# A fourth buffer for float64 words, shared with the later pairs' sums over slots, a third for k's x, one instead of two for turned q: linear attention and an ELU MLP in one launch

## The chip, the cores and the metric

One Trainium2 chip, one core of it. The metric is the device time of one execution in microseconds (us). Nothing is read from an earlier launch; the float64 weights are converted within the launch.

## The reference, cut to what matters

```
def _attn_ref(q, k, v, omega):                 # q, k, v: 8 x 8 x 576 x 64, omega: 128 x 64
    def phi(x):
        proj = np.einsum('bhsd,md->bhsm', x, omega)
        sq = np.sum(x * x, axis=-1, keepdims=True) / 2.0
        h = proj - sq
        h = h - np.max(h, axis=-1, keepdims=True)
        return np.exp(h) / np.sqrt(m)
    q_p, k_p = phi(q * scale), phi(k * scale)
    kv = np.einsum('bhsm,bhsd->bhmd', k_p, v)
    z = np.sum(k_p, axis=2)
    num = np.einsum('bhsm,bhmd->bhsd', q_p, kv)
    den = np.einsum('bhsm,bhm->bhs', q_p, z)[..., None] + 1e-06
    return num / den
...
    x = attn_out.transpose(0, 2, 1, 3).reshape(4608, 512)
    h = x @ w_in                               # 512 x 2048, float64
    g = np.where(h > 0.0, h, np.exp(np.minimum(h, 0.0)) - 1.0)
    return g @ w_out                           # 2048 x 512, float64
```

## The kernel before, in words

Attention is done in 32 **pairs**: a pair is two heads of one batch, so four pairs make a batch of 576 tokens by 512 features. For a pair, `load_pair` has SyncE (SP) load k's x, q's x and v; `project` makes projections on TensorE (PE; `ppk`, `ppq`), takes the least value of each token on VectorE (DVE; `mnk`, `mnq`) and the exponentials on ScalarE (ACT; `hk`, `hq`); `kv` multiplies hk by v on PE (`pkv`); `finish` makes the denominators (PE `pz`, then DVE `junk`, `den`), scales hq by them (the **norm**, L350, on GpSimd, POOL, or on DVE), turns hq on PE (`pt`), copies the turned q to SBUF on ACT (`qh`), multiplies by kv on PE (`pn`) and writes the result as a high part `xh` (ACT) and a low part `xl` (DVE). Pairs 0 to 6 have k in one layout ("native": the squares are taken on the chip by `xk` operations), pairs 7 on have k's x "mixed", where DVE, POOL and ACT split it into `tk` (two halves of 64x576 each) and DVE sums its squares (`sqk`); q's x goes the same way, mixed from pair 8 on (`tq`, `sqq`).

The MLP runs over 12 **blocks** of 384 tokens. A **step** is one of 16 slices of the 2048 inner features for one block: layer 1 is twelve matmuls into the PSUM bank `ph_F` (four chunks of 128 features, each w_high·x_high, w_high·x_low, w_low·x_high; L830 to L832), ACT takes relu and exp (L839, L840), DVE forms `e` (L843), a high and a low part `g` are split off, and layer 2 is nine matmuls (L864 to L866). A chunk is one pair of the batch. Steps 0 to 7 take block 0, for which pairs 0 to 3 must be done; steps 8 to 15 take block 1, half of whose tokens are of batch 1, so that a step's last chunk needs pair 7's xh and xl. `ph` has two banks, shared with other small products, so that layer 1 of step F+2 waits until `e` of step F has been read out of its bank.

The weights come as float64 words. `from_f64` does one 128x512 block in nine instructions: SP loads the words (`raw_w`, L752), ACT makes `u_w` of the upper words (L755) and scales the lower ones (L759), DVE clamps (L763), shifts (L770) and puts in the sign (L775), POOL adds the lower words (L778), a cast makes the high part (`w1c` or `w2h`) and POOL or DVE the low part. There are 16 blocks for each matrix, done for blocks w1_0, w2_0, w1_1 and so on before the steps that need them, mostly before 216 us. `u_w` has three buffers, `raw` three.

The order of all instructions on all engines is made by a planner (`Plan`): each operation has a due time and a planned cost, and whatever is ready, has a buffer and is due first starts next. Buffers of a tag are given out in the order of due times. An operation with an alternative engine goes to whichever would end it first by plan. So a count of buffers changes not only when a tile can be written but the order in which every engine's queue is filled. Names below: `e_7` is `e` of step 7, `tk_8` is tk of pair 8, `u_w2_6` is u of block 6 of the second matrix; a further number is that of the tile.

Of the kernel before, what the change touches and what calls it, by code (L numbers as in the profile page):

```python
# [18 lines left out]
P = 128  # L19
B, H, S, D, M = 8, 8, 576, 64, 128  # L20
# [258 lines left out]
def act(n, psum=False, ptr=False):  # L279
    return (51 if psum else 93) + 0.833 * n + (93 if ptr else 0)  # L280
# [6 lines left out]
def pool(n):  # L287
    return 40 + 2.33 * n
# [3 lines left out]
def performer_elu_kernel(  # L292
# [14 lines left out]
    nc = tc.nc  # L307
# [3 lines left out]
    sb = ctx.enter_context(tc.tile_pool(name="sb", bufs=1))  # L311
# [31 lines left out]
    def copy(e, dst, src):  # L343
        if e == "ACT":
            nc.scalar.copy(dst, src)  # L345
        else:
            nc.vector.tensor_copy(dst, src)  # L347
# [47 lines left out]
    def load_pair(i, due):  # L395
        s = st.setdefault(i, {})

        def dma(dst, src, nbytes, *writes):
            nonlocal due
            op("SP", 500, due, lambda: nc.sync.dma_start(dst(), src), (), writes, nbytes)  # L400
            due += 0.01

        for nm, nat, mixed in (("k", k, kx), ("q", q, qx)):
            if native(i, nm):
                t = s["x" + nm] = Buf(sb, [P, 2, S], F32, "ld" if nm == "k" else "t", f"x{nm}_{i}", 2)
                dma(lambda t=t: t()[0:D], nat[i], P * S * 4, (t, 0), (t, 1))
            else:
                t = s["x" + nm] = Buf(sb, [P, 2, S], F32, "ld", f"x{nm}_{i}", 2)
                dma(lambda t=t: t(), mixed[i - NNAT[nm]], P * S * 8, (t, 0), (t, 3))
        t = s["v"] = Buf(sb, [P, NV], F32, "v", f"v_{i}", 2)  # L410
        dma(lambda: t(), v[i], P * NV * 4, t)
# [168 lines left out]
    def kv_sums(i, due, p, parts):  # L580

        s = st[i]
        h, v, kvf = s["hk"], s["v"], kvs[i % 2]
        z = s["z"] = Buf(sb, [P, 4, M], F32, "zs", f"zs_{i}", 2)
        kvt = Buf(sb, [P, M], F32, "kvt", f"kvt_{i}", 2)

        def mms():
            for t in range(5):
                for a in range(2):
                    j, o = (2 * t + a, (2 * t + a) * (D + 1)) if t < 4 else (8, 8 * (D + 1) + a * (D + 2))  # L590
                    nc.tensor.matmul(  # L591
                        p()[a * D:a * D + D, 0:M], v()[:, o:o + D], h()[:, j, :], start=(t == 0), stop=(t == 4)
                    )

        op("PE", 1260, due, mms, [*parts, v], ((p, 0),))
        op(
            "ACT", act(M, True), due + 2.2, lambda e: copy(e, kvt(), p()[:, 0:M]), ((p, 0),), (kvt,),
            alt=other("kv", "DVE", dve(M)),
        )
        op("PE", 109, due + 2.5, lambda: nc.tensor.transpose(p()[:, M:2 * M], kvt(), ident), (kvt,), ((p, 1),))  # L600
        op(
            "ACT", act(P, True), due + 2.8, lambda e: copy(e, kvf, p()[:, M:2 * M]), ((p, 1),), (("kvf", i % 2),),
            alt=other("kv", "DVE", dve(P)),
        )

        def add(n, d, dst, x, y, reads):
            op("POOL", pool(n), d, lambda: nc.gpsimd.tensor_tensor(dst(), x(), y(), ALU.add), reads, (z,))

        add(4 * M, due + 0.1, lambda: z(), lambda: h()[:, 0:4], lambda: h()[:, 4:8], parts)
        add(2 * M, due + 0.2, lambda: z()[:, 0:2], lambda: z()[:, 0:2], lambda: z()[:, 2:4], (z,))  # L610
        for a in range(2):
            r = slice(a * D, a * D + D)
            add(
                M, due + 0.3 + 0.1 * a, lambda r=r, a=a: z()[r, a], lambda r=r, a=a: z()[r, a],
                lambda r=r: h()[r, 8], [*parts, z],
            )

    def finish(i, due):
# [11 lines left out]
                nc.tensor.transpose(pz()[:, a * P:(a + 1) * P], z()[:, a:a + 1].to_broadcast([P, P]), ident)  # L630

        def sums():
            nc.tensor.matmul(pz()[:, 0:2 * M], ones, z()[:, 0:2].rearrange("p a m -> p (a m)"), start=True, stop=True)  # L633

        if i < NONES:
            op("PE", 220, due - DUE_Z, spread, (z,), (pz,))
        else:
            op("PE", 430, due - DUE_Z, sums, (z,), (pz,))
        qh = Buf(sb, [P, 2, S], F32, "qh", f"qh_{i}", 2)
        for g in range(3):  # L640
            d = due - 9 + g
            js = slice(4 * g, min(4 * g + 4, NJ))
# [86 lines left out]
    def from_f64(src, hi, lo, nm, due, key):  # L729

        raw = Buf(sb, [P, 2 * 512], I32, "raw", f"raw_{nm}", 3)
        u = Buf(sb, [P, 512], F32, "u", f"u_{nm}", 3)

        def words():  # L740
# [12 lines left out]
        op(
            "ACT", act(512), due - 7,
            lambda: nc.scalar.activation(u(), up().bitcast(F32), AF.Copy, scale=2.0 ** -112), ((raw, 1),), (u,),  # L755
        )
        op(
            "ACT", act(512), due - 6.5,
            lambda: nc.scalar.activation(low(), low().bitcast(U32), AF.Copy, scale=2.0 ** -29), ((raw, 0),), ((raw, 0),),  # L759
        )  # L760
        op(
            "DVE", dve(512, True), due - 6,
            lambda e: (nc.vector if e == "DVE" else nc.gpsimd).tensor_scalar(  # L763
                u(), u(), -F64_MAX, F64_MAX, ALU.max, ALU.min
            ),
            (u,), (u,), alt=other("conv_clamp", "POOL", 1885), port=True,
        )
# [248 lines left out]
```

## Time and profile before

| | us |
|---|---|
| median of 3 runs | 1079.98 (1079.9 to 1080.02) |
| the profiled execution's own time | 1078.17 |
| its span, first to last instruction | 1076.3 |
| PE busy in the span | 1050.0 |
| DVE, ACT, POOL busy | 601.5, 731.6, 474.4 |

The span leaves 1.87 us outside the first and last instruction, and the profiled execution is 1.81 us below the median. PE is busy for 98% of the span. In the forty slices of the page PE shows lower digits in the first six slices alone (to about 160 us), and the granted clock is below full there too. The mean clock over the span is 0.990 of 2.4 GHz. What an engine was waiting for is put down by the view of waits to whatever released it last.

### The profile page before, as it was taken

How to read it: one execution, taken by the hardware profiler on the slowest of the kernel's cores; microseconds unless marked ns; L12 is line 12 of the kernel's file. 1: busy time of each engine (PE TensorE's matmuls, PEld its weight loads, DVE VectorE, ACT ScalarE, POOL GpSimd, SP SyncE). 2: the span in 40 equal slices, each digit the busy share in tenths (PEclk: the TensorE clock that was granted, in tenths of full speed). 3: DMA queues.
4: the chain of work that ended last, by engine and by line, in shares of the span. 5: the costliest groups of instructions: out<-in, count | busy, mean ns of one | idle time of the engine just before them, and what ended most of it. 6: DMA issues, size and time to landing. Idle time of an engine off the chain costs nothing.

```text
span 1076.3 us, 19179 instructions
## 1 busy us (share of the span) xinstructions
PE 1050.0 (98%) x6043; PEld 916.2 (85%) x6043; DVE 601.5 (56%) x2343; ACT 731.6 (68%) x1949; POOL 474.4 (44%) x466
## 2 busy tenths in 40 slices
PE   7999699999999999999999999999999999999998
PEld 7777589898888888998888888898888888898987
DVE  5788889755776754235666665224566665322221
ACT  6987775547977985347889998427899988432222
POOL 4677666753443554223454345223344554322221
PEclk8999899999999999999999999999999999999999
DMA  6555477657553553435455545444545542253431
GB/s 196 155 178 191 166 255 258 227 211 234 187 194 128 185 170 128 166 118 168 170 169 156 170 150 177 149 135 134 180 138 177 167 153 98 98 167 131 153 125 62
DMA packets 53237, 176.92 MB, mean 164 GB/s; under 512 B 6032, under 2 KB 6224, under 8 KB 53136
## 3 DMA queue, kind: packets, MB, share of 16 engines
q1 hardware_dynamic: 53136, 175.69, 49.3%
q8 instruction: 49, 0.80, 0.3%
q14 instruction: 52, 0.43, 0.1%
HBM read 155.48 MB, written 20.19 MB: 163 GB/s over the span
## 4 chain that ended last, share of the span: by engine, by line
PE 83%; ACT 5%; DVE 5%; DMA 3%; POOL 2%; issue 2%; SPq 0%; POOLq 0%; DVEq 0%; ACTq 0%
PE acc L864 12%; PE ph L830 11%; PE acc L866 11%; PE acc L865 11%; PE ph L832 11%; PE ph L831 11%; PE ppq L507 2%; PE pt L673 2%; PE pkv L591 2%; PE pn L700 2%; PE ppk L507 2%; DMA xk<-in_kx_dram 1%; PE ppq L457 1%; ACT hk L427 1%; ACT hq L427 1%
## 5 line engine op out<-in xcount | busy, mean ns | idle before, releaser
L350 POOL TENSOR_TENSOR g<-e,g 128x384 fp32r<-128x384 f32 x176 | 186.4, 1059 | 450.5 <-DVE g L347 333.3
L830 PE MATMUL ph<-xh,w1c 128*128 128x384 f32 x768 | 266.6, 347 | 0.8 <-DVE e L843 0.8
L832 PE MATMUL ph<-xh,w1c 128*128 128x384 f32 x768 | 258.3, 336 | 0.0
L831 PE MATMUL ph<-xl,w1c 128*128 128x384 f32 x768 | 258.0, 336 | 0.0
L843 DVE SCALAR_TENSOR_TENSOR e<-e,ph 128x384 f32<-128x384 f32 x192 | 106.2, 553 | 247.5 <-ACT e L840 244.0
L839 ACT ACTIVATE e<-ph 128x384 f32<-128x384 f32 x192 | 94.7, 493 | 216.1 <-PE ph L832 209.7
L864 PE MATMUL acc<-w2h,g 128*128 128x512 f32 x576 | 235.1, 408 | 0.7 <-ACT o L345 0.7
L865 PE MATMUL acc<-w2l,g 128*128 128x512 f32 x576 | 228.3, 396 | 0.0
L866 PE MATMUL acc<-w2h,g 128*128 128x512 f32 x576 | 228.2, 396 | 0.0
L830 PEld LDWEIGHTS ph<-xh,w1c 128*128 128x128 f32 x768 | 144.5, 188 | 15.6 <-issue 5.1
L831 PEld LDWEIGHTS ph<-xl,w1c 128*128 128x128 f32 x768 | 144.6, 188 | 8.0
L832 PEld LDWEIGHTS ph<-xh,w1c 128*128 128x128 f32 x768 | 144.0, 188 | 0.0
L866 PEld LDWEIGHTS acc<-w2h,g 128*128 128x128 f32 x576 | 108.6, 189 | 25.7
L864 PEld LDWEIGHTS acc<-w2h,g 128*128 128x128 f32 x576 | 108.6, 189 | 17.6 <-issue 4.1
L865 PEld LDWEIGHTS acc<-w2l,g 128*128 128x128 f32 x576 | 108.9, 189 | 11.7
L840 ACT ACTIVATE e<-e 128x384 f32<-128x384 f32 x192 | 101.6, 529 | 3.4
L525 DVE CUSTOM_DVE_ANT_0 hq<-ppq,p2q 128x128 f32<-128x128 f32 x216 | 54.1, 288 | 63.4 <-ACT p2q L516 62.4
L350 POOL TENSOR_TENSOR hq<-hq,den 128x512 f32<-128x512 f32 (+1 forms) x93 | 81.0, 884 | 10.2 <-DVE den L661 8.5
L525 DVE CUSTOM_DVE_ANT_0 hk<-ppk,p2k 128x128 f32<-128x128 f32 x225 | 56.3, 287 | 45.6 <-ACT p2k L516 41.1
L652 DVE CUSTOM_DVE_ANT_0 junk<-hq,pz 128x128 f32<-128x128 f32 (+1 forms) x320 | 73.5, 280 | 10.6 <-PE pz L633 8.2
L516 ACT ACTIVATE p2q<-ppq,sqq 128x128 f32<-128x128 f32 x216 | 67.5, 369 | 14.0 <-PE ppq L507 13.3
L516 ACT ACTIVATE p2k<-ppk,sqk 128x128 f32<-128x128 f32 x225 | 67.4, 365 | 7.1 <-PE ppk L507 6.9
(94 smaller groups left out, 1619.5 us busy)
## 6 DMA issues: line engine op xcount, KB each, us to landing
w1c<-w1s SPq DMA_DIRECT2D x176, 512.0 KB, 3.3
raw_w<-in_w_dram SPq DMA_DIRECT2D x32, 512.0 KB, 4.2
xk<-in_kx_dram SPq DMA_DIRECT2D x25, 576.0 KB, 4.2
xq<-in_qx_dram SPq DMA_DIRECT2D x24, 576.0 KB, 4.6
v<-in_v_dram SPq DMA_DIRECT2D x32, 325.0 KB, 3.6
out_dram<-o SPq DMA_DIRECT2D x36, 256.0 KB, 2.6
w1s<-w1c SPq DMA_DIRECT2D x16, 512.0 KB, 3.3
xq<-in_q_dram SPq DMA_DIRECT2D x8, 288.0 KB, 3.9
```

Of the source, the lines that this page charges most:

```text
L350: (nc.vector if e == "DVE" else nc.gpsimd).tensor_tensor(*args)
L516: nc.scalar.activation(p2()[:, a], view()[:, a, M:], AF.Identity, bias=sq()[:, j:j + 1], scale=1.0)
L525: nc.vector.tensor_tensor_reduce(out=h()[:, j, :], in0=view()[:, a, 0:M], in1=p2()[:, a, :], scale=1.0, scalar=HIGHEST, op0=ALU.add, op1=A ...
L830: nc.tensor.matmul(ph(), wh, xh[:, c, o:o + TB], start=(c == 0), stop=False)
L831: nc.tensor.matmul(ph(), wh, xl[:, c, o:o + TB], start=False, stop=False)
L832: nc.tensor.matmul(ph(), wl, xh[:, c, o:o + TB], start=False, stop=(c == NC - 1))
L839: op("ACT", act(TB, True), due, lambda: nc.scalar.activation(e(), ph(), AF.Relu, scale=-1.0), (p,), (e,))
L840: op("ACT", act(TB), due + 0.2, lambda: nc.scalar.activation(e(), e(), AF.Exp, scale=-1.0), (e,), (e,))
L843: lambda: nc.vector.scalar_tensor_tensor(e(), e(), -1.0, ph(), ALU.add, ALU.max), (p, e), (e,),
L864: nc.tensor.matmul(a(), g()[:, 0, ts], w2h[:, f], start=(f == f0), stop=False)
L865: nc.tensor.matmul(a(), g()[:, 0, ts], w2l[:, f], start=False, stop=False)
L866: nc.tensor.matmul(a(), g()[:, 1, ts], w2h[:, f], start=False, stop=(f == f1 - 1))
```

## The change

Four counts of buffers, and where two kinds of tile live. Tag `raw` goes from three to four buffers of 4 KB a partition. For pairs 8 on, z's sums over slots (tag `zs`, two buffers) and the copy of kv before its transpose (`kvt`, two buffers) lose their own buffers and lie in one `raw` tile together. k's x, and q's mixed x which has the same tag `ld`, gets three buffers where it had two. The turned q (`qh`) has one where it had two. No arithmetic is changed, and no operation is added or removed.

```
-                t = s["x" + nm] = Buf(sb, [P, 2, S], F32, "ld" if nm == "k" else "t", f"x{nm}_{i}", 2)
+                t = s["x" + nm] = Buf(sb, [P, 2, S], F32, "ld" if nm == "k" else "t", f"x{nm}_{i}", 3 if nm == "k" else 2)
...
-                t = s["x" + nm] = Buf(sb, [P, 2, S], F32, "ld", f"x{nm}_{i}", 2)
+                t = s["x" + nm] = Buf(sb, [P, 2, S], F32, "ld", f"x{nm}_{i}", 3)
...
-        z = s["z"] = Buf(sb, [P, 4, M], F32, "zs", f"zs_{i}", 2)
-        kvt = Buf(sb, [P, M], F32, "kvt", f"kvt_{i}", 2)
+
+        zt = s["z"] = Buf(sb, [P, 2 * 512], I32, "raw", f"zs_{i}", 4)
+        ktk = (zt, "kvt")
+
+        def z():
+            return zt().bitcast(F32)[:, 0:4 * M].rearrange("p (t m) -> p t m", m=M)
+
+        def kvt():
+            return zt().bitcast(F32)[:, 4 * M:5 * M]
...
-        qh = Buf(sb, [P, 2, S], F32, "qh", f"qh_{i}", 2)
+        qh = Buf(sb, [P, 2, S], F32, "qh", f"qh_{i}", 1)
...
-        raw = Buf(sb, [P, 2 * 512], I32, "raw", f"raw_{nm}", 3)
+        raw = Buf(sb, [P, 2 * 512], I32, "raw", f"raw_{nm}", 4)
```

Through the planner it moves instructions on every engine. Some change engine as well: the norm of pair 7 goes from DVE to POOL, and five halves of tk go from POOL to DVE. The new functions' lines lie 8 further down from `finish` on (L752 is L760 after, L763 is L771, L770 is L778, L843 is L851, L673 is L681, L700 is L708).

SP's queue at the start of the kernel, before (loads of k's x `xk`, q's x `xq`, v, and of words `raw`):

```order
L362 DMA omf_110<-in_omT_dram 64x128 x2
L752 DMA raw_w1_0_121<-in_w1_dram 128x1024
L752 DMA raw_w1_1_123<-in_w1_dram 128x1024
L752 DMA raw_w2_0_132<-in_w2_dram 128x1024
L400 DMA xk_2_139<-in_k_dram 64x1152
L400 DMA xq_2_197<-in_q_dram 64x1152
L400 DMA v_2_207<-in_v_dram 128x650
L400 DMA xk_3_232<-in_k_dram 64x1152
L752 DMA raw_w1_2_281<-in_w1_dram 128x1024
L400 DMA xq_3_310<-in_q_dram 64x1152
L400 DMA v_3_324<-in_v_dram 128x650
L400 DMA xk_4_367<-in_k_dram 64x1152
```

And after, in the same place:

```order
L362 DMA omf_110<-in_omT_dram 64x128 x2
L400 DMA xk_2_121<-in_k_dram 64x1152
L760 DMA raw_w1_0_123<-in_w1_dram 128x1024
L760 DMA raw_w1_1_132<-in_w1_dram 128x1024
L760 DMA raw_w2_0_139<-in_w2_dram 128x1024
L400 DMA xk_3_146<-in_k_dram 64x1152
L760 DMA raw_w1_2_150<-in_w1_dram 128x1024
L400 DMA xq_2_200<-in_q_dram 64x1152
L400 DMA v_2_224<-in_v_dram 128x650
L400 DMA xk_4_245<-in_k_dram 64x1152
L760 DMA raw_w2_1_281<-in_w2_dram 128x1024
```

The load of pair 2's k now stands ahead of the first three blocks of words, pair 3's and the fourth block of words ahead of pair 2's q and v.

DVE's queue from the last denominators of pair 7 on, before (each RECIPROCAL ends a group of denominators; hq_7 scaled by den_7 is the norm of pair 7):

```order
L661 RECIPROCAL den_7_1504<-den_7_1504 128x1
L843 SCALAR_TENSOR_TENSOR e_6_1534<-e_6_1534,ph_6_1480 128x384
L770 TENSOR_SCALAR u_w1_7_1433<-u_w1_7_1433 128x512
L770 TENSOR_SCALAR u_w2_6_1494<-u_w2_6_1494 128x512
L775 SCALAR_TENSOR_TENSOR u_w1_7_1433<-raw_w1_7_1397,u_w1_7_1433 128x512
L775 SCALAR_TENSOR_TENSOR u_w2_6_1494<-raw_w2_6_1443,u_w2_6_1494 128x512
L350 TENSOR_TENSOR hq_7_1414<-hq_7_1414,den_7_1504 128x512 x2
L350 TENSOR_TENSOR hq_7_1414<-hq_7_1414,den_7_1504 128x128
L350 TENSOR_TENSOR g_6_1557<-e_6_1534,g_6_1557 128x384
L763 TENSOR_SCALAR u_w2_7_1516<-u_w2_7_1516 128x512
```

And after:

```order
L669 RECIPROCAL den_7_1501<-den_7_1501 128x1
L347 CAST w2h_79<-u_w2_5_1343 128x512
L347 CAST w1c_7_1546<-u_w1_7_1445 128x512
L771 TENSOR_SCALAR u_w2_6_1532<-u_w2_6_1532 128x512
L350 TENSOR_TENSOR tk_8_1456<-xk_8_918,tk_8_1456 64x576
L778 TENSOR_SCALAR u_w2_6_1532<-u_w2_6_1532 128x512
L350 TENSOR_TENSOR tk_9_1488<-xk_9_1234,tk_9_1488 64x576
L783 SCALAR_TENSOR_TENSOR u_w2_6_1532<-raw_w2_6_1308,u_w2_6_1532 128x512
L851 SCALAR_TENSOR_TENSOR e_6_1557<-e_6_1557,ph_6_1527 128x384
L525 ISA hk_8_1580,mnk_8_1581<-ppk_8_0_1563,p2k_8_0_1571 128x128
```

The norm is gone from DVE, and halves of pair 8's and pair 9's tk stand there now, ahead of e_6.

PE's queue around the turn of pair 7 (`pt_7`), before (ppk_8 are the projections of pair 8's k, pn_7 pair 7's last product):

```order
L507 MATMUL ppk_8_0_1554<-om_75,tk_8_1389 128x256 x2
L507 MATMUL ppk_8_1_1559<-om_75,tk_8_1389 128x256 x2
L673 MATMUL pt_7_0_1576<-ident_67,hq_7_1414 128x128 x4
L673 MATMUL pt_7_1_1588<-ident_67,hq_7_1414 128x128 x4
L673 MATMUL pt_7_2_1601<-ident_67,hq_7_1414 128x128
L507 MATMUL ppk_8_2_1609<-om_75,tk_8_1389 128x256 x2
L700 MATMUL pn_7_0_1615<-qh_7_1584,kvf1_78 64x256 x2
L700 MATMUL pn_7_256_1618<-qh_7_1584,kvf1_78 64x320 x2
L507 MATMUL ppk_8_3_1641<-om_75,tk_8_1389 128x256 x2
L507 MATMUL ppk_8_4_1645<-om_75,tk_8_1389 128x256
L830 MATMUL ph_7_1651<-xh_83,w1c_7_1625 128x384
```

And after (all of ph_7 and nine matmuls of ph_8 stand ahead of the first row):

```order
L507 MATMUL ppk_8_3_1660<-om_75,tk_8_1456 128x256 x2
L507 MATMUL ppk_8_4_1664<-om_75,tk_8_1456 128x256
L681 MATMUL pt_7_0_1670<-ident_67,hq_7_1421 128x128 x4
L838 MATMUL ph_9_1679<-xh_83,w1c_9_1555 128x384
L839 MATMUL ph_9_1679<-xl_84,w1c_9_1555 128x384
L840 MATMUL ph_9_1679<-xh_83,w1c_9_1555 128x384
L838 MATMUL ph_9_1679<-xh_83,w1c_9_1555 128x384
L839 MATMUL ph_9_1679<-xl_84,w1c_9_1555 128x384
L840 MATMUL ph_9_1679<-xh_83,w1c_9_1555 128x384
L681 MATMUL pt_7_1_1695<-ident_67,hq_7_1421 128x128 x4
L681 MATMUL pt_7_2_1700<-ident_67,hq_7_1421 128x128
```

Layer 1 of steps 7, 8 and part of 9 has moved ahead of pair 7's last product, which stands five rows further on: after three more matmuls of ph_9 and two of ppk_9.

## Rows read from the trace of the kernel before

**Rows 1.** Busy time by stretch: from to in us, length, then busy us and instructions (x) of PE, its weight loads, DVE, ACT, POOL, then granted clock, DMA share and GB/s. 62.40 is where pair 3's xl ends, 145.00 just after e_7, 216.00 where the conversions are about done.

```profile
16.90:62.40 45.50, 41.01 (x312) 34.20 (x311) 35.91 (x141) 41.01 (x118) 32.09 (x30) 0.96 0.50 152
62.40:145.00 82.60, 70.65 (x418) 57.43 (x418) 69.56 (x226) 66.65 (x172) 54.42 (x41) 0.92 0.56 186
145.00:216.00 71.00, 69.89 (x353) 62.83 (x352) 61.57 (x100) 42.29 (x84) 48.95 (x38) 1.00 0.72 253
216.00:1076.30 860.30, 856.18 (x4893) 750.39 (x4891) 425.99 (x1862) 572.65 (x1555) 334.32 (x351) 1.00 0.47 154
```

**Rows 2.** Waits of PE: total us, times, longest; the first row of 54 to 216 us, the second of 216 us to the end.

```profile
PE pt L673 <- DVE hq L350: 4.5, 2, 3.4
...
PE ppq L507 <- ACT xh L345: 0.2, 1, 0.2
```

**Rows 3.** Busy time by stretch again, for two stretches of 9 us.

```profile
126.00:135.00 9.00, 4.22 (x20) 2.74 (x20) 8.41 (x21) 5.30 (x14) 4.38 (x4) 0.78 0.65 238
135.00:144.00 9.00, 8.65 (x42) 6.94 (x40) 8.08 (x20) 8.16 (x22) 5.43 (x4) 0.84 0.55 201
```

**Rows 4.** Waits of SP's queue, 0 to 216 us, the longest.

```profile
SPq L752 <- POOL u_w L778: 48.2, 20, 5.4
```

**Rows 5.** Groups of ACT's instructions from 16.9 to 62.4 us: count (x), busy us, mean ns of one, idle before.

```profile
L427 ACT ACTIVATE hq<-ppq,mnq 128x128 f32<-128x128 f32 x35 | 10.1, 370 | 1.4 <-DVE mnq L465 1.2
...
L436 ACT ACTIVATE xk<-xk 64x576 f32<-64x576 f32 x7 | 4.7, 680 | 1.6 <-DMA xk<-in_k_dram 1.5
L759 ACT ACTIVATE raw_w<-raw_w 128x512 int32<-128x512 uint32 x6 | 4.1, 680 | 0.0
L755 ACT ACTIVATE u_w<-raw_w 128x512 f32<-128x512 f32 x5 | 3.4, 684 | 0.2 <-DMA raw_w<-in_w_dram 0.2
...
L345 ACT COPY kvf<-pkv 128x128 f32<-128x128 f32 x4 | 1.2, 288 | 1.1 <-DVE z L347 1.1
```

**Rows 6.** Timeline of DVE: start, us, line, operation, count. The first row is pair 3's xl, the second the last reciprocals of pair 7, the third e_7.

```profile
61.61 0.82 DVE L713 TENSOR_TENSOR xl<-pn,xh 128x256 fp32r<-128x256 f32 x2 [0.44 <-ACT xh L345]
...
124.72 0.23 DVE L661 RECIPROCAL den<-den 128x4 f32<-128x4 f32 x2
...
143.99 0.56 DVE L843 SCALAR_TENSOR_TENSOR e<-e,ph 128x384 f32<-128x384 f32 x1
```

**Rows 7.** Groups of DVE's and POOL's instructions by shape, 54 to 216 us.

```profile
L770 DVE TENSOR_SCALAR u_w<-u_w 128x512 int32<-128x512 int32 x27 | 21.2, 793 | 0.7 <-POOL u_w L763 0.6
L775 DVE SCALAR_TENSOR_TENSOR u_w<-raw_w,u_w 128x512 int32<-128x512 int32 x26 | 18.4, 718 | 0.0
L763 DVE TENSOR_SCALAR u_w<-u_w 128x512 f32<-128x512 f32 x21 | 15.5, 740 | 2.5 <-ACT u_w L755 2.5
L843 DVE SCALAR_TENSOR_TENSOR e<-e,ph 128x384 f32<-128x384 f32 x26 | 14.2, 548 | 5.5 <-ACT e L840 5.4
L350 DVE TENSOR_TENSOR g<-e,g 128x384 fp32r<-128x384 f32 x13 | 10.3, 791 | 0.0
L347 DVE CAST g<-e 128x384 fp32r<-128x384 f32 x12 | 9.4, 783 | 1.5 <-PE acc L866 0.5 <-DVE e L843 0.5
L347 DVE CAST w2h<-u_w 128x512 fp32r<-128x512 f32 x16 | 7.3, 458 | 0.0
...
L347 DVE CAST w1c<-u_w 128x512 fp32r<-128x512 f32 x9 | 6.4, 712 | 0.5 <-PE ph L832 0.5
L350 DVE TENSOR_TENSOR tk<-xk,tk 64x576 fp32r<-64x576 f32 x5 | 5.8, 1151 | 0.1
...
L525 DVE CUSTOM_DVE_ANT_0 hk<-ppk,p2k 128x128 f32<-128x128 f32 x22 | 5.5, 284 | 3.3 <-ACT p2k L516 3.2
L350 DVE TENSOR_TENSOR hq<-hq,den 128x512 f32<-128x512 f32 x2 | 3.5, 1776 | 0.0
...
L479 DVE TENSOR_REDUCE sqk<-xk 128x9 f32<-128x576 f32 x4 | 3.0, 744 | 0.6 <-ACT xk L476 0.6
...
L350 POOL TENSOR_TENSOR hq<-hq,den 128x512 f32<-128x512 f32 x7 | 7.9, 1130 | 0.9 <-PE ph L832 0.7 <-DVE den L661 0.2
```

**Rows 8.** Timeline of PE: a pn of pair 6, the last work ahead of pair 7's turn, the turn, then ph_9's first matmuls and two of layer 2. Bracketed is the idle time ahead and what ended it; the distance of two starts is what one costs in a row of them.

```profile
114.67 1.19 PE L700 MATMUL pn<-qh,kvf 128*64 128x256 f32 x8
...
125.98 0.63 PE L507 MATMUL ppk<-om,tk 128*128 128x256 f32 x4
130.02 0.66 PE L673 MATMUL pt<-ident,hq 128*128 128x128 f32 x4 [3.40 <-DVE hq L350]
...
144.61 0.44 PE L830 MATMUL ph<-xh,w1c 128*128 128x384 f32 x1 [0.39 <-DVE e L843]
144.88 0.33 PE L831 MATMUL ph<-xl,w1c 128*128 128x384 f32 x1
145.05 0.34 PE L832 MATMUL ph<-xh,w1c 128*128 128x384 f32 x1
...
148.49 0.39 PE L864 MATMUL acc<-w2h,g 128*128 128x512 f32 x1
148.72 0.40 PE L865 MATMUL acc<-w2l,g 128*128 128x512 f32 x1
```

**Rows 9.** The shift of the conversion (L770) by itself, 0 to 216 us: least, median and greatest ns.

```profile
L770 DVE TENSOR_SCALAR u_w<-u_w x30: 407/424/1540, 16.8 to 214.6; 128x512 int32<-128x512 int32 x30
```

More of the change, by code (lines that the diff above doesn't have):

```diff
@@ L596, in kv_sums @@
         op(
-            "ACT", act(M, True), due + 2.2, lambda e: copy(e, kvt(), p()[:, 0:M]), ((p, 0),), (kvt,),
+            "ACT", act(M, True), due + 2.2, lambda e: copy(e, kvt(), p()[:, 0:M]), ((p, 0),), (ktk,),
             alt=other("kv", "DVE", dve(M)),
         )
-        op("PE", 109, due + 2.5, lambda: nc.tensor.transpose(p()[:, M:2 * M], kvt(), ident), (kvt,), ((p, 1),))
+        op("PE", 109, due + 2.5, lambda: nc.tensor.transpose(p()[:, M:2 * M], kvt(), ident), (ktk,), ((p, 1),))
         op(
@@ L606, in add @@
         def add(n, d, dst, x, y, reads):
-            op("POOL", pool(n), d, lambda: nc.gpsimd.tensor_tensor(dst(), x(), y(), ALU.add), reads, (z,))
+            op("POOL", pool(n), d, lambda: nc.gpsimd.tensor_tensor(dst(), x(), y(), ALU.add), reads, (zt,))
         add(4 * M, due + 0.1, lambda: z(), lambda: h()[:, 0:4], lambda: h()[:, 4:8], parts)
-        add(2 * M, due + 0.2, lambda: z()[:, 0:2], lambda: z()[:, 0:2], lambda: z()[:, 2:4], (z,))
+        add(2 * M, due + 0.2, lambda: z()[:, 0:2], lambda: z()[:, 0:2], lambda: z()[:, 2:4], (zt,))
         for a in range(2):
@@ L614, in kv_sums @@
                 M, due + 0.3 + 0.1 * a, lambda r=r, a=a: z()[r, a], lambda r=r, a=a: z()[r, a],
-                lambda r=r: h()[r, 8], [*parts, z],
+                lambda r=r: h()[r, 8], [*parts, zt],
             )
@@ L632, in sums @@
         def sums():
-            nc.tensor.matmul(pz()[:, 0:2 * M], ones, z()[:, 0:2].rearrange("p a m -> p (a m)"), start=True, stop=True)
+            nc.tensor.matmul(pz()[:, 0:2 * M], ones, z().bitcast(F32)[:, 0:2 * M], start=True, stop=True)
         if i < NONES:
```

## The prediction

> **What bounds the kernel now.** I read the busy time by stretch first [rows 1]. From 216 us to the end PE is busy for 856.18 of 860.3 us at full clock, and the one wait of its own in the view of waits there is 0.2 us [rows 2]. Nothing that buffers decide can be gained there; only harm can come of it. Up to 216 us PE has idle time: 4.5 us in 16.9 to 62.4, 12.0 in 62.4 to 145, 1.1 in 145 to 216. So the change is worth what it does before about 145 us. Two stretches matter.
>
> The opening, to 62.4 us, is ACT's: it is busy 41.01 of 45.5 us [rows 1], and pair 3, the last that step 0 needs, ends there with its xl on DVE, which waited for ACT's xh [rows 6]. ACT's waits for loads in it are 1.5 us for xk and 0.2 for words [rows 5]. SP's queue waits 48.2 us in all to load words, for POOL's last read of a raw buffer [rows 4].
>
> The middle, 62.4 to 145, has DVE busy 69.56 of 82.6 and PE 70.65 [rows 1]. The longest gap of PE is 3.40 us at 130.02, for the norm of pair 7 on DVE [rows 2, 8]; the granted clock is 0.78 and 0.84 in the 18 us from 126 [rows 3], so a part of them is at the lower of the two levels, after PE had been idle. Then ph_9 waits for e_7 at 144.61, which DVE reached at 143.99 [rows 6, 8]. After it PE hardly stops again, so the time of the end is: when DVE comes to e_7, and how much of the work of the opening and the middle PE still owes then.
>
> **The opening.** With a third buffer of k's x, SP loads pair 2's k ahead of three blocks of words and pair 3's k ahead of pair 2's q and v. ACT's queue ahead of pair 3's first xh, by the orders, has one more q or k square and one more low-word operation (0.68 + 0.68), and two fewer squares, four fewer exponentials of pair 4 and one copy of kvf (1.36 + 4 x 10.1/35 + 0.29 = 2.81), the rest cancelling: 1.36 - 2.81 = -1.45 us [rows 5]. If the waits for xk and for words went too, 1.7 us more [rows 5], so 3.1 us at the most. At the least it is 0: pair 2's load stands in front of the words now, so words come later by a transfer, and a wait for words can take the place of one for xk. I take x = 2.0, the queue's 1.45 and a third of the 1.7, nearer to the upper end because ACT is 90% busy there and its queue is what counts [rows 1].
>
> **DVE up to e_7.** Between the last reciprocals of pair 7 and e_7 DVE needed 143.99 - 124.95 = 19.0 us before [rows 6]. After, there stand in that place: casts of w2h and w1c (0.46 + 0.71), two clamps and one more of u_w2_8 (3 x 0.74), three shifts (3 x 0.79), two signs (2 x 0.72), three halves of tk (3 x 1.15), e_6 (0.55), six of hk_8 (6 x 0.28), one g (0.79) and one sum of squares (0.74): 14.4 us [rows 7]. That is 4.6 us less. What went out is the norm (two of 1.78 and a short one, 3.8 us), which POOL does in 1.13 each [rows 7], pair 7's xl, and some casts. But ahead of pair 7's reciprocals there is more in DVE's queue than before: net of what cancels, a clamp and a shift (0.74 + 0.79), a sign (0.72), a cast of w1c (0.71), two g (0.79 + 0.78) and a sum of squares (0.74), less a cast of w2h (0.46): 4.8 us [rows 7]. So e_7 has 4.8 - 4.6 = 0.2 us more DVE work ahead of it, the same within what means can tell.
>
> DVE comes earlier to e_7 only by idle time that it loses on the way. From the opening this is x. In the middle it had 82.6 - 69.56 = 13.0 us idle [rows 1], of which 2.5 us was one wait for ACT's u_w and 5.4 us waits for ACT's exp ahead of e [rows 7]. With four raw buffers more words are ready, and conversion steps can stand where DVE waited. Call it y: between 0 (the waits only move) and 2.5 + 5.4 = 7.9. I take 2.5, the wait that the fourth buffer answers directly; the waits for exp hang on PE and ACT.
>
> **What PE owes at e_7.** Ahead of ph_9 PE no longer has five matmuls of pair 7's turn (5 x 0.66/4 = 0.8), pair 7's pn (1.2), nine of layer 2 (9 x 0.23 = 2.1) and three of ph_8 (3 x 0.17 = 0.5): 4.6 us that it still has to do when e_7 comes [rows 8]. In exchange PE has ph_7 and most of ph_8 to do where it waited 3.4 us for the norm, so that wait goes; but what it wins there it meets again at e_7, since DVE is no earlier by it.
>
> **Other edits.** One buffer of turned q costs nothing by the orders: in both of them pair i's pn stands ahead of pair i+1's turn on PE; without that cover a pair would cost one pn, 1.2 us [rows 8]. z's sums and kvt in a raw buffer: pairs 8 on begin these when the last words are being read, near 216 us, and PE there waits for nothing [rows 2]; a word load that now waits for pair 8 would delay one w2 block, bounded by the longest raw wait, 5.4 us [rows 4], and covered by the margin of DVE (425.99 of 860.3 busy) [rows 1]. I put 0 for both. Five halves of tk that go from POOL to DVE are counted above or lie behind e_7, where DVE has the margin.
>
> **The sum.** Moved end = 0.2 + 4.6 - x - y = 4.8 - 2.0 - 2.5 = +0.3 us. Profiled execution 1078.17 + 0.3 = 1078.5; the median of the runs is 1.81 above the profiled one, so 1080.3 us. What a measurement can tell from no change is about 0.2%, 2.16 us: under 1077.8 is faster, over 1082.1 slower. The clock adds to the upper end alone: the lower level between 126 and 144 cost 9 x (0.22 + 0.16) = 3.4 us of PE time [rows 3], at work that was not all on the path; should PE now wait for e_7 with 4.6 us of work behind it, the same 3.4 us falls on the path. Ends: 4.8 - 3.1 - 7.9 = -6.2 (1073.8) and 4.8 + 3.4 = +8.2 (1088.2).
>
> **Rivals.**
> A, forecast: gain of the opening and of the norm is paid back at ph_9. 1080.3, its own range 1077.8 to 1082.1.
> B, faster: DVE's idle time in the middle closes, since words are always there. For it: SP's 48.2 us of waiting on raw buffers [rows 4], and e_6, which now stands behind seven other operations and so need not be waited for. Waits for exp gone alone: 4.8 - 2.0 - 5.4 = -2.6 (1077.4); with the wait for u_w, 4.8 - 2.0 - 7.9 = -5.1 (1074.9). Against it: words come through u_w as well, whose buffers stay three. I take 1076 for it.
> The Trainium skill, page "Perfetto Trace Analysis", section "Optimization Strategy", says that the same gap repeated on the engine that should be busy can mean too few buffers for the next tile; by it B would be the outcome. The waits of SP's queue look like that, but they are not PE's own.
> C, slower: DVE's queue at pair 7. If y is 0, because tk_8 and tk_9 in front of e_6 wait for their own inputs as long as DVE waited before, the end moves by 4.8 - 2.0 = +2.8, and with half of the clock's 3.4 by +4.5: 1084.5. It decides from the point where y is under about 0.7. For it: ph_6 to ppk_8_0 on PE need the second half of tk_8, which stands behind two casts and a clamp after pair 7's denominators. Against it: DVE has no lack of other work in between.
> D, slower: DVE's shifts meet POOL. The same instruction takes 407 to 1540 ns with a median of 424 and a mean of 793 in the middle [rows 7, 9]: some are held up by 1.1 us. The norm of pair 7 is on POOL now, near four clamps and shifts of DVE; two more held up cost 2.2 us on DVE, and the end moves by 0.3 + 2.2 = +2.5: 1082.8.
> The Trainium skill, page "SBUF — State Buffer", section "Who interferes with whom", says that DVE's second pair of ports is GpSimd's too and is locked for a whole instruction, and that tensor_scalar can be such a one; the trace's two kinds of shifts agree with this rule.
> E, it doesn't do what it says: the fourth raw buffer and the third of k's x bring no transfer forward that anyone waits for (x = y = 0), and the order moves anyway: +4.8, 1085.1.
>
> **Chances.** A 0.34, B 0.33, C 0.23, D 0.05, E 0.05. A is the likeliest single case, so its 1080.3 is the predicted time. Faster 0.33, within 0.2% 0.34, slower 0.33. The range takes in both ends of the sum, within a microsecond: 1073.5 to 1088.
>
> **What would show it.** The opening: pair 3's xl ends 2 us ahead of 62.4, and ACT's wait for xk is under 1 us. The middle: the norm row of pair 7 is POOL's, PE's wait for it is gone, the wait ahead of ph_9 for e_7 is longer than 0.39 us, e_7 starts near 139.7 (143.99 + 0.2 - 2.0 - 2.5), and DVE is idle for about 10.5 us in place of 13.0 from pair 3 to e_7. From 216 us on PE's waits stay under 1 us. SP's raw waits fall well under 48 us if B's ground holds. The forecast is wrong if e_7 comes before 137 (then B), after 142 (C or E), or if pair 8's z or a word load shows as a wait of PE behind 200 us.

## The result: slower by half a per cent, and the profile after

The changed kernel takes 1085.39 us (median of 6 runs) beside 1079.94 us for the kernel before: a ratio of 1.0053, 95% interval 1.0035 to 1.0070. Run again beside the last experiments it was 1.0046 (1.0027 to 1.0065). The profiled execution took 1083.9 us with a span of 1082.0, 5.7 us above that of before. Single profiles of one kernel differ by some microseconds (last section), so the ratio is what counts.

Busy time by stretch, changed kernel, columns as in [rows 1]:

```profile
16.90:62.40 45.50, 42.74 (x343) 35.76 (x343) 37.17 (x147) 42.29 (x123) 34.27 (x29) 1.00 0.55 160
62.40:145.00 82.60, 70.03 (x406) 56.03 (x406) 73.89 (x226) 63.29 (x166) 54.16 (x44) 0.92 0.59 200
145.00:216.00 71.00, 66.37 (x330) 58.45 (x329) 55.23 (x96) 41.66 (x86) 38.05 (x28) 1.00 0.65 223
216.00:1082.00 866.00, 858.28 (x4913) 754.95 (x4911) 436.01 (x1877) 571.69 (x1549) 337.01 (x355) 1.00 0.47 154
```

Idle time of PE, taken from the length less its busy time: 2.8 us in the opening (4.5 before), 12.6 in the middle (12.0 before), 4.6 from 145 to 216 (1.1 before), 7.7 from 216 on (4.1 before). The loss lies behind 145 us, where the kernel before had next to no waits. In this pair of profiles it is not the clock's: the granted clock is 0.92 in the middle and 1.00 behind it in both [rows 1].

Timeline of DVE, changed kernel: pair 3's xl, and e_7.

```profile
58.90 0.82 DVE L721 TENSOR_TENSOR xl<-pn,xh 128x256 fp32r<-128x256 f32 x2 [0.47 <-ACT xh L345]
...
138.50 0.54 DVE L851 SCALAR_TENSOR_TENSOR e<-e,ph 128x384 f32<-128x384 f32 x1
```

Pair 3 is done 2.7 us sooner and e_7 begins 5.5 us sooner than in [rows 6]. The norm of pair 7 runs on POOL, and PE's wait of 3.40 us for it is gone. Then PE's waits, changed kernel, 145 to 236 us:

```profile
PE acc L872 <- ACT o L345: 3.0, 3, 1.6
PE ppq L507 <- DVE mnk L525: 2.4, 1, 2.4
PE ph L838 <- DVE e L851: 1.7, 3, 0.8
PE ph L838 <- ACT xh L345: 1.0, 1, 1.0
PE ph L839 <- DVE xl L721: 0.4, 1, 0.4
```

Of these the kernel before has one behind 150 us, 0.7 us for an output. Where they lie, on PE's timeline of the changed kernel:

```profile
178.70 0.44 PE L838 MATMUL ph<-xh,w1c 128*128 128x384 f32 x1 [0.49 <-DVE e L851]
183.48 0.44 PE L838 MATMUL ph<-xh,w1c 128*128 128x384 f32 x1 [0.36 <-DVE e L851]
188.71 0.45 PE L838 MATMUL ph<-xh,w1c 128*128 128x384 f32 x1 [0.80 <-DVE e L851]
195.75 0.50 PE L872 MATMUL acc<-w2h,g 128*128 128x512 f32 x1 [1.58 <-ACT o L345]
...
222.84 0.48 PE L507 MATMUL ppq<-om,tq 128*128 128x256 f32 x2 [2.35 <-DVE mnk L525]
...
232.97 0.50 PE L872 MATMUL acc<-w2h,g 128*128 128x512 f32 x1 [0.42 <-ACT o L345]
234.89 0.50 PE L872 MATMUL acc<-w2h,g 128*128 128x512 f32 x1 [0.96 <-ACT o L345]
```

In step ends, from the traces with the orders laid over them, the changed kernel against before: the last layer 1 matmul of step 2 is 2.2 us earlier, of step 3 3.1 later, of step 7 4.2 earlier, of step 10 0.9 later, of step 16 0.8, of step 17 1.5, of step 19 3.1, of step 21 4.2 us later.

What delays e there is seen in DVE's timeline of the changed kernel. The first and last rows are e of steps 15 and 16; between them stand a clamp, a cast and a shift (left out), the low part of g, and the sign of a conversion:

```profile
178.11 0.54 DVE L851 SCALAR_TENSOR_TENSOR e<-e,ph 128x384 f32<-128x384 f32 x1
...
179.58 1.65 DVE L350 TENSOR_TENSOR g<-e,g 128x384 fp32r<-128x384 f32 x1
181.15 1.81 DVE L783 SCALAR_TENSOR_TENSOR u_w<-raw_w,u_w 128x512 int32<-128x512 int32 x1
182.89 0.54 DVE L851 SCALAR_TENSOR_TENSOR e<-e,ph 128x384 f32<-128x384 f32 x1
```

On ACT the exponential of step 16 was done long before:

```profile
179.62 0.53 ACT L848 ACTIVATE e<-e 128x384 f32<-128x384 f32 x1
```

And POOL's two instructions there, each of which began just before one of DVE's:

```profile
179.40 1.42 POOL L350 TENSOR_TENSOR w2l<-u_w,w2h 128x512 fp32r<-128x512 f32 x1 [1.76 <-DVE w2h L347]
180.78 1.64 POOL L786 TENSOR_TENSOR u_w<-u_w,raw_w 128x512 int32<-128x512 int32 x1
```

So e's input was ready at 180.2, and e_16 stood 2.7 us behind two instructions that were held up beside POOL's: alone, g's low part takes 0.55 us (at 189.50, say) and the sign 0.68 (at 163.66). DVE's distance from e to e is 4.8 us here; a step of PE, twelve matmuls at 0.175 and nine at 0.23, is 4.2.

### The profile page after: what moved, and what is told of

Its sections match the earlier page's. It is cut to its first block, busy times and chain, and to the rows that moved or that the text cites. A ratio compares the mean times of both kernels' runs of the same rounds, so it can differ in the third digit from the quotient of the medians.

```text
span 1082.0 us, 19127 instructions
## 1 busy us (share of the span) xinstructions
PE 1049.3 (97%) x6043; PEld 916.3 (85%) x6043; DVE 609.8 (56%) x2358; ACT 726.8 (67%) x1939; POOL 466.5 (43%) x461
## 4 chain that ended last, share of the span: by engine, by line
PE 83%; ACT 5%; DVE 3%; DMA 3%; POOL 3%; issue 2%; SPq 0%; POOLq 0%; ACTq 0%; DVEq 0%
PE ph L838 11%; PE acc L872 11%; PE acc L873 11%; PE ph L839 11%; PE ph L840 11%; PE acc L874 11%; PE pn L708 3%; PE pt L681 3%; PE ppq L507 3%; PE pkv L599 2%; PE ppk L507 2%; ACT hk L427 1%; POOL u_w L786 1%; PE ppq L457 1%; POOL w2l L350 1%
## 5 line engine op out<-in xcount | busy, mean ns | idle before, releaser
L851 DVE SCALAR_TENSOR_TENSOR e<-e,ph 128x384 f32<-128x384 f32 x192 | 106.1, 553 | 250.6 <-ACT e L848 239.5
L350 POOL TENSOR_TENSOR hq<-hq,den 128x512 f32<-128x512 f32 (+1 forms) x96 | 87.5, 927 | 17.0 <-DVE den L669 16.3
L427 ACT ACTIVATE hk<-hk,mnk 128x128 f32<-128x128 f32 x225 | 71.8, 402 | 0.7 <-DVE mnk L525 0.4
```

The lines of the kernel that those rows point to most:

```text
L350: (nc.vector if e == "DVE" else nc.gpsimd).tensor_tensor(*args)
L427: nc.scalar.activation(h()[:, j, :], src(j), AF.Exp, bias=mn()[:, j:j + 1], scale=-1.0)
L851: lambda: nc.vector.scalar_tensor_tensor(e(), e(), -1.0, ph(), ALU.add, ALU.max), (p, e), (e,),
```

## The experiments

E1 to E4, E5 to E8 and E9 to E12 each ran on one chip beside the kernel before, and the ratios are to the kernel before on the same chip. A median is of 10 or 12 executions, of E5 of 4 and of E10 of 5.

| run | what | median us | ratio (95%) |
|---|---|---|---|
| E1 | order of before, 4 raw | 1080.5 | 1.0006 (0.9984 to 1.0028) |
| E2 | order of before, 3 of k's x | 1074.18 | 0.9964 (0.9944 to 0.9985) |
| E3 | changed, g's low parts on POOL | 1083.45 | 1.0036 (1.0017 to 1.0055) |
| E4 | changed, 4 u | 1082.67 | 1.0037 (1.0014 to 1.0059) |
| E5 | 4 raw alone, own order | 1088.01 | 1.0087 (1.0055 to 1.0119) |
| E6 | 3 of k's x alone, own order | 1079.49 | 1.0001 (0.9989 to 1.0013) |
| E7 | sharing alone, own order | 1078.11 | 0.9987 (0.9972 to 1.0002) |
| E8 | E2 and 4 u | 1073.59 | 0.9952 (0.9935 to 0.9968) |
| E9 | order of before, all new buffers | 1075.01 | 0.9964 (0.9950 to 0.9977) |
| E10 | E9 and 4 u | 1074.76 | 0.9955 (0.9939 to 0.9970) |
| E11 | changed, 4 u, e first | 1078.23 | 0.9987 (0.9969 to 1.0006) |
| E12 | changed, again | 1084.16 | 1.0046 (1.0027 to 1.0065) |

My theory after the result was that the buffers cost nothing and the order that the planner makes of them does. The rival was that a buffer does harm by itself, as earlier loads or a shared raw buffer might.

**The buffers without the order.** The class of buffers gets a second count that the planner alone sees, so that every engine's queue stays as it was:

```
-    def __init__(self, pool, shape, dtype, tag, name, n):
+    def __init__(self, pool, shape, dtype, tag, name, n, plan=None):
...
-                    slots.setdefault(b.key, [0.0] * b.n)
+                    slots.setdefault(b.key, [0.0] * b.plan)
...
-        raw = Buf(sb, [P, 2 * 512], I32, "raw", f"raw_{nm}", 3)
+        raw = Buf(sb, [P, 2 * 512], I32, "raw", f"raw_{nm}", 4, 3)
```

E1 is this, with one turned q:

> The kernel before with every instruction in its old order, planned for three buffers of raw words, but four in SBUF (and one turned q, whose order is the same with one or two). Theory (the order lost the time): raw loads start earlier, SP's wait for raw buffers falls from 48 us to under 30, and the time stays within 0.2% of before, 1078 to 1082. Rival (the buffers themselves cost, since earlier loads collide with others): 1083 or more.

No change that can be measured, though SP's wait for raw buffers fell from 48.2 to 15.6 us. E2 does the same for k's x (3, planned as 2), with three raw buffers and one turned q:

> The kernel before in its old order, planned for two buffers of k's x, three in SBUF, one turned q. Theory (the order lost the time): within 0.2% of before, ACT's wait for xk in the opening (1.5 us) goes down, pair 3's xl no more than 1.5 us earlier than 62.4. Rival (the opening's gain is the buffer's and not the order's): pair 3's xl at 60 or before. Second rival (earlier loads collide): 1083 or more.

Faster by 0.36%. Pair 3's xl ended at 60.5 us and e_7 began at 141.3 (143.99 before), and this lead was kept: the span was 1072.9. ACT's waits in the opening, E2, have no load among them now (1.5 us for xk in [rows 5]):

```profile
ACT hq L427 <- DVE mnq L465: 2.0, 3, 1.0
ACT kvf L345 <- DVE z L347: 0.5, 1, 0.5
ACT qh L345 <- PE pt L673: 0.3, 1, 0.3
```

That is more than the theory allowed and what the first rival said: the buffer wins by itself, though its mark of 60 us was missed by half a microsecond. E9 takes all of the change's buffers in the old order; the shared tile is planned under its old tag (`Buf(..., "raw", f"zs_{i}", 4, 2, "zs")`), with a `kvt` that only the planner sees:

> All of the change's buffers in SBUF (four of raw words that z's sums and the copy of kv share, three of k's x, one turned q), with every engine's queue in the order of before: the planner is told the old counts. Theory (the whole loss is the order's, and the buffers by themselves win what the third buffer of k's x won): 1072 to 1076, as with that buffer alone. Rival (the shared raw buffer costs when z's sums of pair 8, made at 154 us in the old order, hold one of four through the conversions): 1078 or more, SP's waits for raw buffers above the 67 us of the run with three of k's x.

0.9964: the same gain as E2. PE's waits from 145 to 260 us, E9, are one row, and SP's wait for raw buffers is 36.2 us where it was 48.2 [rows 4]:

```profile
PE acc L872 <- ACT o L345: 0.6, 1, 0.6
```

```profile
SPq L760 <- POOL u_w L786: 36.2, 12, 7.9
```

So the change's buffers are worth 0.36%, and the order that came with them costs about 0.9%: E9 and the changed kernel have the same buffers in SBUF and do the same work, and only the order differs, with the engines that it gives some instructions.

**One part at a time, with its own order.** E5 has four raw buffers and one turned q, the rest as before; E6 three of k's x and one turned q; E7 the shared tile among three raw buffers.

> The kernel before with four raw buffers (and one turned q), the planner's own new order; z's sums keep their buffers, k's x keeps two. Theory (what lost the time is the order that the fourth raw buffer brings: conversions drawn ahead of e and of the outputs, pair 8's work drawn ahead into 145 to 235 us): 1082 to 1086, with PE waits of 3 us or more behind 145 us. Rival (it is not raw's): 1078 to 1082, PE's waits behind 145 us under 2 us.

> The kernel before with three buffers of k's x (and one turned q), the planner's own new order. Theory (the gain of the old order with three buffers is there in a new order too, since pair 7's last product stays ahead of ph_9): pair 3's xl at 59 to 60.5, 1073 to 1077. Rival (any new order loses as much as the buffer wins, or third buffer's order draws pair 9's work ahead): 1080 or more.

> The kernel before with z's sums and the copy of kv in one of three raw buffers, all other counts as before. The order is that of before up to about step 16. Theory (sharing costs nothing by itself, pair 8's sums only move behind the last words): 1078 to 1082, PE's waits from 200 to 260 us under 1 us. Rival (sums that wait for a raw buffer hold up pair 8 and with it PE, as the 3.7 us of waits from 216 to 235 us in the changed kernel might): 1082 or more, with waits of PE at 216 to 260 us.

E5 has the highest ratio, from four executions, and its interval overlaps with the changed kernel's. Its waits of PE for e from 145 to 260 us are longer than the changed kernel's 1.7 us:

```profile
PE ph L830 <- DVE e L843: 4.4, 5, 1.5
```

and it loses in the middle as well: step 2 ends 3.6 us earlier than before, step 4 8.9 later. The fourth raw buffer's order harms; the buffer (E1) does not. E6 fell to its rival: pair 3's xl was at 60.5 us, but e_7 began 1.1 us later than before, so the order that came with the third buffer gave back in the middle what the buffer won. By what, I did not take apart: the granted clock of the middle is 0.86 in E6 too, where E2 has 0.92. E7 agrees with its theory: sharing, with its own order, costs nothing that can be measured.

**What in the new order costs, from 160 to 200 us.** First I took g's low part away from DVE in steps 11 to 17, by giving the planned task another engine at issue:

```
-            self.tasks[n][2](eng)
+            self.tasks[n][2](self.fix.get(n, eng))
```

> The changed kernel with its order, but the low parts of g of steps 11 to 17 on POOL in place of DVE. Theory (from 160 to 190 us DVE is the bound, because each of its two-input instructions is held up by 1.1 us beside POOL's, 4.75 us for a step where PE needs 4.17): DVE's time for a step falls under 4.2, the waits of PE for e of 178 to 189 us go, steps 17 to 21 are 2 to 3.5 us earlier, and the time is 1081.5 to 1083.5. Rival (POOL becomes the bound with one more instruction of 1.06 us for a step): PE waits for g or w2l in place of e, 1085 or more.

Neither came out. The time is at the upper end of the theory's range but can't be told from the changed kernel's; step 10 to step 21 took 49.1 us (48.1 in the changed kernel, 49.2 in E12, which is the same kernel, 44.9 before); and PE still waited for e, 2.0 us in all ahead of steps 17 to 19, and not for g or w2l as the rival had it. Two stretches of E3, with POOL (fifth busy time) near full at 8.07 and 7.68 of 9 us:

```profile
171.00:180.00 9.00, 7.71 (x40) 6.64 (x38) 8.93 (x11) 4.94 (x11) 8.07 (x7) 1.00 0.65 224
180.00:189.00 9.00, 8.30 (x42) 7.22 (x42) 7.82 (x11) 4.70 (x10) 7.68 (x6) 1.00 0.88 281
```

and of the changed kernel, where DVE (third) has next to no idle time:

```profile
171.00:180.00 9.00, 8.51 (x44) 7.55 (x43) 9.00 (x13) 5.36 (x10) 5.47 (x5) 1.00 0.71 259
180.00:189.00 9.00, 7.83 (x39) 6.51 (x38) 8.79 (x11) 3.90 (x8) 5.41 (x4) 1.00 0.73 259
```

PE is idle for 2.0 us of the 18 in E3 and for 1.7 in the changed kernel.

E4 gave u, whose three buffers block outputs share with the conversions, a fourth (planned as three):

> The changed kernel with its order, planned for three buffers of u (which block outputs o share), four in SBUF. Theory (conversions of w2_9 on start late, at 158.8 us, because three outputs of block 0 hold all of u): u_w2_9 starts by 157, DVE's wait for it falls from 4.0 us to under 2.5, and the time falls by 1 to 2 us, 1083 to 1084.5. Rival (ACT's queue holds it up, where a low-word operation that waits for its load stands ahead): u_w2_9 stays at 158 or later, 1085.

The profile shows the output's wait of 1.58 us gone, and steps 19 to 21 took 8.4 us in place of 10.3, but not for the reason given: DVE's wait for u_w at 159 us grew from 4.0 to 4.9 us. The waits for e remained:

```profile
178.57 0.45 PE L838 MATMUL ph<-xh,w1c 128*128 128x384 f32 x1 [1.38 <-DVE e L851]
183.35 0.44 PE L838 MATMUL ph<-xh,w1c 128*128 128x384 f32 x1 [0.34 <-DVE e L851]
```

By time alone E4 can't be told from the changed kernel. E11 keeps u's fourth buffer and lets e of steps 13 to 19 go ahead of up to two DVE instructions in front of it that it does not depend on; nothing else moves on any engine:

```
         done = self.order()
+        for n in self.early:
+            k = next(i for i, d in enumerate(done) if d[0] == n)
+            for i in [i for i in range(k) if done[i][1] == "DVE"][:-3:-1]:
+                if not any(done[i][0] in self.tasks[d[0]][3] for d in done[i + 1:k + 1]):
+                    done.insert(k, done.pop(i))
+                    k -= 1
```

> The changed kernel in its new order with four buffers of u (planned as three), and on DVE e of steps 13 to 19 ahead of the two conversion or low-part instructions that stood in front of it. Theory (PE's waits for e from 170 to 190 us come from e standing behind two instructions that POOL holds up by 1.1 us each, not from too much work on DVE): PE's waits for e in steps 14 to 20 go, step 21 ends about 1 us behind the kernel before (it was 4.2 behind in the changed kernel), and the time is 1079 to 1082. Rival (DVE has too much work there whatever its order): the waits move to later steps or to outputs, 1083 or more.

0.9987, level with before, where E4 was 1.0037. From step 10 to step 21 it takes 45.3 us, where E4 takes 47.1 and the kernel before 44.9. Of PE's waits for e one of 0.3 us is left, ahead of step 20. PE in E11, the same two stretches, is full:

```profile
171.00:180.00 9.00, 9.00 (x47) 8.07 (x47) 8.73 (x13) 4.16 (x8) 6.49 (x5) 1.00 0.67 210
180.00:189.00 9.00, 9.00 (x47) 8.25 (x46) 7.48 (x13) 4.13 (x8) 5.36 (x4) 1.00 0.86 297
```

and DVE's instructions are held up still, but behind e and not in front of it:

```profile
177.33 0.56 DVE L858 SCALAR_TENSOR_TENSOR e<-e,ph 128x384 f32<-128x384 f32 x1
177.80 1.00 DVE L357 TENSOR_TENSOR g<-e,g 128x384 fp32r<-128x384 f32 x1
178.73 1.79 DVE L790 SCALAR_TENSOR_TENSOR u_w<-raw_w,u_w 128x512 int32<-128x512 int32 x1
```

They are held up less, too. E11's groups of g's low parts and signs from 162 to 192 us have smaller means than the changed kernel's 1496 and 1323 ns (shown below):

```profile
L357 DVE TENSOR_TENSOR g<-e,g 128x384 fp32r<-128x384 f32 x7 | 9.1, 1295 | 0.0
L790 DVE SCALAR_TENSOR_TENSOR u_w<-raw_w,u_w 128x512 int32<-128x512 int32 x7 | 7.0, 1000 | 0.0
```

So E11 shows that e's place in DVE's queue costs PE its waits; how much of the gain is the place and how much the shorter holds that followed is not shown.

Step 21 itself was 3.0 us behind before, not 1, since this execution was 2.7 behind at step 10 already. E12, the changed kernel again, has the same granted clock as E11 in the first 17 us (0.90) and in the middle (0.88): E11's span is 6.6 us shorter than E12's, 0.7 of it by step 10, 4.0 in steps 10 to 21 and 2.0 behind. That agrees with the medians, 1078.23 and 1084.16.

**A better kernel, and the changed one again.** E8 is E2 with a fourth u, E10 is E9 with it:

> The kernel before in its old order with three buffers of k's x in SBUF, one turned q, and four buffers of u, planned as three. Theory (outputs of a block wait for a buffer of u behind the conversions, which cost 2 us in the changed kernel): ACT's waits for POOL's w2l ahead of outputs (0.6 and 1.35 us) go, and it is 0 to 2 us faster than three buffers of k's x alone, 1072 to 1075. Rival (outputs were not on the path in the old order, where PE has no wait for them behind 150 us): the same as with three buffers of k's x alone.

> As the run before it, with four buffers of u in SBUF, planned as three. Theory: the fourth buffer of u adds 0 to 1 us to the gain, 1072 to 1075; it is the fastest version so far or level with it. Rival: its space buys nothing behind 60 us.

> The changed kernel as it is, beside the versions above on one chip. Both theories: 1083 to 1088, a ratio near 1.005.

E8 (0.9952) and E10 (0.9955) beat both kernels; their intervals overlap with those of E2 and E9, so the fourth u is not shown to be worth anything there. In their profiles steps 10 to 21 take 44.0 us, so 1.3 of E11's 45.3 are still the new order's. E12 repeats the result.

## Why the prediction was wrong, by its own steps

The forecast was no change, 1080.3 us; it came out 5.1 us slower than that, inside the range, on the side of the slower rivals but by none of their mechanisms. That it lies inside the range is luck: the upper end was made of x = y = 0 and of a lower clock, and neither came.

**The opening, x = 2.0:** right in size, but not in its parts. Pair 3's xl was 2.7 us earlier. The prediction gave 1.45 of its 2.0 to ACT's shorter queue and the rest to loads; in E2 the buffer alone, with the old queue, does 1.9 us, with ACT's waits for loads gone.

**DVE up to e_7:** right in the number, by luck. Forecast at 139.7, measured at 138.50. Busy time from the end of pair 3's xl to the end of e_7, before and after:

```profile
62.43:144.55 82.12, 70.22 (x416) 57.01 (x415) 69.14 (x224) 66.20 (x171) 54.39 (x41) 0.92 0.56 186
59.72:139.04 79.32, 67.73 (x401) 54.56 (x399) 70.83 (x220) 60.63 (x160) 51.93 (x41) 0.91 0.56 191
```

DVE had 1.7 us more work (0.2 was forecast) and 4.5 us less idle time (y = 2.5 was forecast), so two errors cancel. And y had no ground: [rows 7] run to 216 us, and of their waits for ACT's u_w (2.5) and for exp (5.4) only 0.6 us lie in the middle. DVE's waits there, before, 62.43 to 144.55 us:

```profile
DVE mnq L465 <- PE ppq L457: 4.1, 6, 1.8
...
DVE e L843 <- ACT e L840: 0.6, 3, 0.2
```

and after, 59.72 to 139.04 us:

```profile
DVE mnq L465 <- PE ppq L457: 0.3, 1, 0.3
```

What went were above all the waits for PE's projections. The norm on POOL took PE's wait away, as said; but PE did not meet that wait again at e_7, where it waited 0.41 us (0.39 before).

**What PE owes at e_7, 4.6 us:** right, but 1.9 us of new waits came on top. From ph_9's first matmul to ph_10's last PE took 14.2 us (139.10 to 153.3) where it took 7.7: 6.5 more, 4.6 of it owed work and the rest pair 7's product, which now waited on the path (0.93 for qh, 0.97 for xh, 0.42 for xl, less the 0.45 that went for e). At step 10 the balance was +0.9 us; the sum had said +0.3. That they lie so close is luck as well: in E3, E4, E11 and E12, which have the same queues up to there, it was -2.8, -0.1, +2.7 and +3.4.

**"After it PE hardly stops again", and 0 for what lies behind e_7:** this is the step that failed, with all of the measured loss but 0.9 us in it. From the end of step 10 to that of the last step the changed kernel took 4.9 us longer than the kernel before, and E12 7.5; E1, E2, E8, E9 and E10, in the old order, took from 1.7 us less to 1.1 more. The prediction had itself named the sign: PE's waits behind 216 us were to stay under 1 us, and they were 4.2. I took PE's lack of waits in the kernel before for a property of the stretch ("DVE has the margin"), and counted work queued ahead of e up to step 10 only. But the change moved every queue far beyond: the two orders differ as far as step 150, which ends near 880 us.

Three things cost PE there. In 160 to 190 us e stood behind two held-up instructions for each step (1.65 us of PE's waits), at 195.75 an output waited for a buffer of u behind the conversions (1.58), where the kernel before has one of 0.7, and from 216 to 235 us there are 3.7 us more of waits. I put these down to work of pairs 8 and 9, drawn ahead into the last conversions, which no run shows. Steps 21 to 36 took 4.5 us longer than before, and 2.8 of that came back by the last step. E4 and E11 show the first two: with both gone, steps 10 to 21 take 45.3 us. The third stays open; its wait for mnk is in E11 as well (2.7 us), while its waits for outputs (0.42 and 0.96) are down to 0.15 in E12 and belong in part to the one execution.

**Rival D** had the mechanism, with a chance of 0.05 and at the wrong place: DVE's instructions are held up by 1.1 us beside POOL's, but it cost PE at steps 11 to 17 and not at pair 7. Groups of DVE's instructions of the changed kernel from 159 to 190 us:

```profile
L350 DVE TENSOR_TENSOR g<-e,g 128x384 fp32r<-128x384 f32 x7 | 10.5, 1496 | 0.0
L783 DVE SCALAR_TENSOR_TENSOR u_w<-raw_w,u_w 128x512 int32<-128x512 int32 x7 | 9.3, 1323 | 0.0
...
L771 DVE TENSOR_SCALAR u_w<-u_w 128x512 f32<-128x512 f32 x7 | 3.6, 514 | 4.0 <-ACT u_w L763 4.0
```

and of the kernel before from 156 to 190 us:

```profile
L763 DVE TENSOR_SCALAR u_w<-u_w 128x512 f32<-128x512 f32 x7 | 7.6, 1102 | 0.0
L770 DVE TENSOR_SCALAR u_w<-u_w 128x512 int32<-128x512 int32 x7 | 5.1, 742 | 0.0
L350 DVE TENSOR_TENSOR g<-e,g 128x384 fp32r<-128x384 f32 x7 | 4.9, 702 | 0.0
...
L775 DVE SCALAR_TENSOR_TENSOR u_w<-raw_w,u_w 128x512 int32<-128x512 int32 x7 | 4.7, 678 | 0.0
```

Both orders lose about the same to POOL, some 11 and 12 us in these stretches: the one on clamps (7 x 0.69 us above the 0.41 of one alone), shifts (7 x 0.33) and others, the other on g's low parts and signs (7 x 0.95 and 7 x 0.65). So the amount hardly differs between these two, but what stands behind a held-up instruction does: e of steps 15 to 17 began 2.7, 2.7 and 4.6 us after ACT's exponential had ended in the changed kernel, 1.4, 0.0 and 0.5 us before the change, and 0.0 each in E11, where the same groups lose 7.5 us. The Trainium skill, page "SBUF — State Buffer", section "Who interferes with whom", says that a DVE instruction with two inputs in SBUF contends with a GpSimd instruction that reads SBUF; the rows agree, 1.65 and 1.81 us in place of 0.55 and 0.68.

**Rivals B, C, E:** B's ground was sound (e_7 was 5.5 us earlier, SP waited 39.5 in place of 48.2 us for raw buffers) but the lead was spent on owed work. C and E were wrong: e_7 came sooner, not later, and that their times (1084.5 and 1085.1) are near the measured one is luck. D's and E's times count the forecast's 0.3 us twice; by their own sums they are 1082.5 and 1084.8. **Sharing and one turned q at 0:** right; E7 is 0.9987, and E1, E2 and E9 have one turned q in the old order and are not slower.

## What to carry to other kernels

Where a planner sets the order, a buffer count is two changes: when a tile can be filled, and the whole order behind it. Time them apart, by giving the memory the new count and the planner the old one; here the first was worth -0.36% and the second about +0.9%. And a stretch without waits in the trace of before is no evidence that it stays so when its queues are reshuffled: count what stands ahead of each released result (here e) on its in-order engine for as far as the order moves, with the durations that it has beside the other engine.

## What the runs showed of the hardware that was not expected

The first 17 us are not the same from one execution to the next: in some profiles the granted clock was 0.90 there (a mean, with the lower of the two levels in part of the stretch) and in others 1.00, with the same instructions queued. The kernel before, first stretch:

```profile
0.00:16.90 16.90, 12.29 (x76) 11.36 (x77) 8.46 (x18) 8.99 (x24) 4.57 (x9) 0.90 0.75 226
```

E1, in the same order, same stretch:

```profile
0.00:16.90 16.90, 13.61 (x87) 12.58 (x88) 9.29 (x20) 9.99 (x26) 4.52 (x9) 1.00 0.83 243
```

PE was busy for 1.3 us longer there. E1 has one raw buffer more, but the changed kernel (0.90) and E3 (1.00) differ in the same way with the same buffers. In these two, whose queues are the same up to step 10, pair 3's xl ended at 59.7 and 58.2 us, and the profiled executions of the changed kernel and of E12, the same program, have spans of 1082.0 and 1087.0 us. The middle (62.4 to 145 us) differs too, with a granted clock of 0.92 in the changed kernel and E3 and of 0.88 in E4, E11 and E12. The balance at step 10 goes with both: -2.8 us at 1.00 and 0.92 (E3), -0.1 at 1.00 and 0.88 (E4), +0.9 at 0.90 and 0.92 (changed), +2.7 and +3.4 at 0.90 and 0.88 (E11, E12). Steps 10 to 21, at full clock, scatter far less: 44.9 us in the kernel before, E1, E2 and E9. So a difference of a few microseconds between the spans of two single profiles of this kernel says nothing; the ratios over many runs do, and so do waits that are there in one order in each of its profiles and in the other in none. PE's waits for e ahead of steps 17 to 19 are such: the changed kernel, E3, E4, E5 and E12 have all three, and the kernel before, E1, E2, E8, E9 and E10 have none.
